# Attention with two exponential engines: own exponential buffers, more VectorE sets, and a sliding activity floor

## The chip, the cores and the metric

The kernel runs on one core of one Trainium2 chip. Its time is the device time of one execution in microseconds (us); the median of several executions is given. The profile is one execution taken by the hardware profiler. Its engines are TensorE (PE: matmuls, with weight loads shown apart as PEld), VectorE (DVE), ScalarE (ACT), GpSimd (POOL) and SyncE (SP). Each has its own instruction queue, and the instructions of a queue run in the order in which they were written. SBUF is the on-chip memory of 128 partitions, PSUM the memory into which TensorE writes, here eight banks of 512 float32 columns.

## The reference

For x of 2048 rows and 640 columns (bfloat16) the kernel computes a gated mix of an attention and a dense layer:

```python
g = sigmoid((x * gate_w).sum(-1, keepdims=True))
# A: 32 heads of 20 columns
q, k, v = split(x @ wqkv)
a = softmax(q @ k.T * 20 ** -0.5) @ v   # per head, 2048 x 2048 scores
a = concat(a) @ wo
# B: 640 -> 1536 -> 640
h = x @ w1 + b1
b = (h * tanh(softplus(h))) @ w2        # Mish
out = g * a + (1 - g) * b
```

The 32 heads have 2048 x 2048 scores each, 134 million exponentials in all, and they are the largest single piece of work.

## The kernel before

**Units, groups and sets.** A group G is a set of four heads (p, eight of these) with one chunk of 512 queries (qc, four of these), so there are 32 groups. In a group the keys come in 16 blocks of 128 (j). A unit is one head, one key block and 512 queries: a matmul of 32 rows (a head's 20 columns padded to 32, line 1051) writes the scores of 128 keys by 512 queries into one PSUM bank. Units are taken in order, alternately three and two at a time (`WIDTHS`), into two PSUM tiles S0 (three banks) and S1 (two banks). ScalarE then takes one exponential of the whole tile (`emit_exp`, line 1061) and writes it as bfloat16 into an SBUF tile E. The four units of one key block form a set: four matmuls of 21 columns (20 of V and one of ones, line 1107, `emit_set`) add into the single PSUM accumulator `acc`. After 16 sets a group is finished, and VectorE transposes the accumulator (line 1076), divides by the sums and transposes back.

The E tiles of both widths come from one pool `ep` with four buffers of 1536 columns. An exponential may write when the PV matmuls (line 1107) that read the tile four exponentials back are done.

**JV sets.** In the groups of `JV_GROUPS` (4 to 30 except multiples of 4, 20 groups) the last key block does not go to ScalarE. Its four score matmuls (line 682, `jv_chain`) write into ordinary PSUM banks, VectorE takes each over into `E_dve` (line 691), and seven VectorE operations on 2048 columns (lines 710 to 732, `jv_steps`) compute the exponential from its bits and a polynomial. The PV matmuls of this set (with `VB` as weights) are placed by `emit_jv` when the planner holds the result for ready. There is one `E_dve`, so a group's JV set has to be multiplied before the next group's is started.

**Other work.** The projections for Q, K and V, the dense layer with its Mish function, the output projection and a test of bounds are cut into chains: a list of matmul pieces, and an eviction by VectorE at the end. All share two PSUM banks (pool `pp`). The Mish of each of 48 tiles has an exponential on ScalarE (line 502) and a chain of VectorE operations.

**Order.** The order is written out by hand in the program itself, by a planner that runs while the kernel is built. It keeps an estimated time for each engine (`T`). For each exponential i it writes the scores of i + 1, the exponential i, the PV sets that are ready (`emit_pv`), VectorE steps that are due (`run_slow`) and then calls `pump`. That takes pieces of the chains in the order of their due times, hard ones 12 exponentials ahead of soft ones. [...]

**Filler matmuls.** `pump` also writes matmuls without use (`busy_matmul`, line 992), which multiply a constant tile `busy` (128 x 512 ones) by itself into a bank that is free. Their number is set by an account `owed`: each exponential adds 0.56 of 446 ns for each unit, less weights for its score and PV matmuls; every piece or filler takes its cost off. Above 110 ns something is written.

Of the kernel before, what the change touches and what calls it, by code (L numbers as in the profile page):

```python
# [9 lines left out]
P = 128  # L10
# [3 lines left out]
BF16 = mybir.dt.bfloat16  # L14
# [2 lines left out]

class Chain:  # L20

    def __init__(self, start, due, pieces, finish, ready=None, hard=True, bank=None):
        self.start, self.due, self.pieces, self.finish = start, due, deque(pieces), finish
        self.ready = ready or (lambda: True)
        self.hard = hard
        self.bank = bank
        self.fresh = True
        self.cost = sum(c for c, _ in pieces)  # L30

# [8 lines left out]
def attention_with_maximum(tc, A_wqkv, b_dram, out2d, xT, VA, wo_sb, g_t, ident, pool):  # L40
# [10 lines left out]
    with tc.For_i(0, H, 1, name="heads") as h:  # L51
# [20 lines left out]
        with tc.For_i(0, S, P, name="queries") as q0:  # L72
            q = pool["m"].tile([P, P], BF16, tag="e", name="q")
            nc.vector.tensor_copy(out=q[0:DH, :], in_=qT[0:DH, bass.ds(q0, P)])
            s0 = pool["s"].tile([P, 3 * QC], F32, tag="S0", name="s0")
            s1 = pool["s"].tile([P, QC], F32, tag="S1", name="s1")
            for c in range(S // QC):
                nc.tensor.matmul(
                    (s0[:, c * QC : (c + 1) * QC] if c < 3 else s1[:, :]),
                    lhsT=q[0:DH, :], rhs=kT[0:DH, c * QC : (c + 1) * QC], start=True, stop=True,  # L80
                )
            mx = pool["m"].tile([P, 4], F32, tag="r", name="mx")
            nc.vector.tensor_reduce(out=mx[:, 0:1], in_=s0, op=ALU.max, axis=X)
            nc.vector.tensor_reduce(out=mx[:, 1:2], in_=s1, op=ALU.max, axis=X)
            nc.vector.tensor_tensor(out=mx[:, 2:3], in0=mx[:, 0:1], in1=mx[:, 1:2], op=ALU.max)
            nc.vector.tensor_scalar(
                out=mx[:, 3:4], in0=mx[:, 2:3], scalar1=-scale, scalar2=None, op0=ALU.mult
            )
            e0 = pool["e"].tile([P, 3 * QC], BF16, tag="E", name="e0")
            e1 = pool["e"].tile([P, QC], BF16, tag="E", name="e1")  # L90
            for e, sc in ((e0, s0), (e1, s1)):
                nc.scalar.activation(e[:, :], sc[:, :], ACT.Exp, bias=mx[:, 3:4], scale=scale)
            eT = pool["stage"].tile([P, NS, P], BF16, tag="stage", name="eT")
            for b in range(0, NS, 8):
                ps = pool["pp"].tile([P, 8, P], BF16, tag="pp", name="ps")
                for j in range(8):
                    k = (b + j) * P
                    src = e0[:, k : k + P] if k < 3 * QC else e1[:, k - 3 * QC : k - 3 * QC + P]
                    nc.tensor.transpose(ps[:, j, :], src, ident)
                nc.vector.tensor_copy(out=eT[:, b : b + 8, :], in_=ps[:, :, :])  # L100
            o = pool["acc"].tile([P, DH + 1], F32, tag="acc", name="o")
            for j in range(NS):
                nc.tensor.matmul(
                    o[:, :], lhsT=eT[:, j, :], rhs=vh[:, j, :], start=(j == 0), stop=(j == NS - 1)
                )
            on = pool["m"].tile([P, DH], BF16, tag="h", name="on")
            rec = pool["t"].tile([P, 1], F32, tag="rec", name="rec")
            nc.vector.reciprocal(out=rec, in_=o[:, DH : DH + 1])
            nc.vector.tensor_scalar(
                out=on, in0=o[:, 0:DH], scalar1=rec, scalar2=None, op0=ALU.mult  # L110
            )
            nc.sync.dma_start(out=o_dram[bass.ds(q0, P), bass.ds(col, DH)], in_=on)

    with tc.For_i(0, NS, 1, name="rows") as s:
        op = pool["e"].tile([P, H, 32], BF16, tag="E", name="op")
        nc.vector.memset(op, 0.0)
        rows = bass.ds(s * P, P)
        nc.sync.dma_start(
# [5 lines left out]
        for p in range(NQ):  # L124
            nc.tensor.transpose(
                ps[:, p, :], op[:, 4 * p : 4 * p + 4, :].rearrange("p h d -> p (h d)"), ident
            )
        oT = pool["e"].tile([P, NQ, P], BF16, tag="E", name="oT")
        nc.vector.tensor_copy(out=oT[:, :, :], in_=ps[:, :, :])
        a = pool["s"].tile([P, 2, QC], F32, tag="S1", name="a")  # L130
        for half in range(2):
# [5 lines left out]
                )  # L137
        g = pool["t"].tile([P, 1], F32, tag="rec", name="g")
        nc.vector.tensor_copy(out=g, in_=g_t[:, bass.ds(s, 1)])
        ot = pool["e"].tile([P, 2, D // 2], BF16, tag="E", name="ot")  # L140
        nc.vector.scalar_tensor_tensor(
            out=ot[:, :, :], in0=a[:, :, 0 : D // 2], scalar=g,
            in1=bt.rearrange("p (a c) -> p a c", a=2), op0=ALU.mult, op1=ALU.add,
# [5 lines left out]
def kernel(  # L149
# [25 lines left out]
    LN2 = 0.6931471805599453  # L175
    Q_SCALE = 512.0 * float(DH) ** -0.5 / LN2
    WIDTHS = (3, 2)
    JV_GROUPS = [G for G in range(4, 31) if G % 4 != 0]
    JV_BIAS = 32
    N_CAP = 1.0e9  # L180
    NCELL = 48
    CELLS_KEPT = 2
# [12 lines left out]
    wsp = ctx.enter_context(tc.tile_pool(name="wsp", bufs=2))  # L195
    ktp = ctx.enter_context(tc.tile_pool(name="ktp", bufs=2))
    qtp = ctx.enter_context(tc.tile_pool(name="qtp", bufs=3))
    ep = ctx.enter_context(tc.tile_pool(name="ep", bufs=4))
    tp = ctx.enter_context(tc.tile_pool(name="tp", bufs=1))
    mp = ctx.enter_context(tc.tile_pool(name="mp", bufs=2))  # L200
    outp = ctx.enter_context(tc.tile_pool(name="outp", bufs=2))
# [12 lines left out]
    wkp = [consts.tile([P, KT, 4, 32], BF16, tag=f"wkp{i}", name=f"wkp{i}") for i in range(2)]  # L214
    T2 = [consts.tile([P, QC], BF16, tag=f"T2_{i}", name=f"T2_{i}") for i in range(2)]
    cells = [consts.tile([P, QC], BF16, tag=f"cell{i}", name=f"cell{i}") for i in range(NCELL)]
    busy = consts.tile([P, QC], BF16, tag="busy")
    xn = consts.tile([P, NQC], F32, tag="xn")
    wn = consts.tile([P, NQ, 2], F32, tag="wn")
    vn = consts.tile([P, 3], F32, tag="vn")  # L220
# [139 lines left out]
    def open_bank():  # L360
        T["pe"] = max(T["pe"], bank_free.popleft())
        bank_free.append(T["pe"])

    spare = [None]

# [310 lines left out]
    def jv_chain(G, p, t, start, due):  # L676
        box = {}
        bank = opener(box, QC)

        def piece():  # L680
            jv_free[0] = False
            nc.tensor.matmul(  # L682
                bank()[:, :],
                lhsT=kT[p][32 * t : 32 * t + 32, JV * P : (JV + 1) * P],
                rhs=qT[G][32 * t : 32 * t + 32, :],
                tile_position=(32 * t, 0),
            )

        def finish():
            evac(690)  # L690
            nc.vector.tensor_scalar(  # L691
                out=E_dve.bitcast(I16)[:, t, :], in0=box["ps"][:, :], scalar1=ROUND,
                scalar2=ROUND - 512.0 * JV_BIAS, op0=ALU.add, op1=ALU.subtract,
            )
            if t == 3:
                left = (it_at(G + 1) - now[0]) * 1115.0
                steps(T["dve"], jv_steps(G), T["act"] + left - 4000.0)

        def ready():
            return G in qT and (jv_free[0] if t == 0 else not jv_free[0])  # L700

        return Chain(start, due, [(215, piece)], finish, ready, bank=bank)

    def jv_steps(G):
        V = nc.vector
# [166 lines left out]
    for G, (p, qc) in enumerate(groups):  # L872
        if with_jv[G]:
            for t in range(4):
                x = it_at(G) + 3 + 3 * t
                chains.append(jv_chain(G, p, t, x, x + 3))

    def spread(a, b, n):
        return [(a + (b - a) * k / n, a + (b - a) * (k + 1) / n) for k in range(n)]
# [67 lines left out]
        ], x + 12, x + 24,  # L947
    ))
    chains.append(bound_chain(it_at(27), it_at(28)))
    chains.sort(key=lambda ch: (ch.due - (12 if ch.hard else 0), ch.start))  # L950
    shares = list(chains)

    current = [None]
    done = [0.0]
    BURST = 700.0
    UNIT = 446.0
    FLOOR = 0.56
    W_QK, W_PV = 0.5, 1.1
    AHEAD = 1500.0

    def run_piece():
        ch = current[0]
        cost, fn = ch.pieces.popleft()
        fn()
        T["pe"] += cost
        ch.fresh = False
        done[0] += cost
# [12 lines left out]
    def urgent(i):  # L980
        if current[0] is not None and current[0].hard and current[0].due <= i + 1:
            return True
        return any(ch.hard and ch.due <= i + 1 for ch in chains)

    def busy_matmul(ch):
        if ch is None:
            spare[0] = take_bank()
# [1 line left out]
        else:  # L989
            ps = ch.bank()  # L990
        n = ps.shape[1]
        nc.tensor.matmul(ps[:, 0:n], lhsT=busy[:, 0:P], rhs=busy[:, 0:n], start=True, stop=True)  # L992
        T["pe"] += n / 2.4
        return n / 2.4

    owed = [0.0]

    def pump(i, sets):
        want = sum(ch.share(i + 1) for ch in shares)
        if i >= 8:  # L1000
            owed[0] += FLOOR * UNIT * iters[i][1] - 215.0 * (W_QK + W_PV * sets)

        limit = T["act"] + NS_EXP[iters[min(i + 1, NI - 1)][1]] - NS_SCORES_SEEN - 60.0
        spent = 0.0
        while True:
# [2 lines left out]
            ch = current[0]  # L1008
            soon = ch is not None and urgent(i)
            must = soon or (ch is not None and done[0] < want and spent < BURST)  # L1010
            if not must and owed[0] < 110.0:
                break
            if not soon and (T["pe"] + 215.0 > limit or ((ch is None or ch.fresh) and not bank_ready())):
                break
# [4 lines left out]
            else:  # L1019
                break  # L1020
            spent += cost
            owed[0] = max(owed[0] - cost, -300.0)
        owed[0] = min(owed[0], 400.0)

    def run_later(i):
        go = sorted(x for x in later if x[0] <= i)
# [13 lines left out]
    def emit_qk(i):  # L1040
# [4 lines left out]
        S_of[i] = ps  # L1045
        T["pe"] = max(T["pe"], S_free.get(tag, 0.0))
        S_full[i] = T["pe"] + NS_SCORES_SEEN
        T["pe"] += NS_SCORES
        for k in range(n):
            G, p, qc, j, t = units[a + k]  # L1050
# [6 lines left out]

    def emit_exp(i):
        a, n = iters[i]
        E = ep.tile([P, max(WIDTHS) * QC], BF16, tag="E", name="E")  # L1060
        nc.scalar.activation(  # L1061
            E[:, 0 : n * QC], S_of.pop(i)[:, 0 : n * QC], ACT.Exp, scale=LN2 / 512.0
        )
# [39 lines left out]
    def emit_set(G, p, qc, j, moving, full, VB=None):  # L1103
        n = pv_sets[0]
        T["pe"] = max(T["pe"], full, T["acc"] if n == 0 else 0.0) + NS_SET
        for t in range(4):
            nc.tensor.matmul(  # L1107
                acc[32 * t : 32 * t + DH + 1, :],
# [54 lines left out]
    ]  # L1163
    def spin_up(n):
        for _ in range(n):
            nc.tensor.matmul(acc[:, :], lhsT=busy[:, 0:P], rhs=busy[:, :], start=True, stop=True)

    def first_proj(w, dst, ps, c0, n, eng):
        for kt in range(KT):
# [117 lines left out]
    with tc.If(ok == 0):  # L1287
        attention_with_maximum(
            tc, A_wqkv, b_dram, out2d, xT, VA, wo_sb[0], g_t, ident,
            dict(s=spool, acc=accpool, pp=pp, k=ktp, q=qtp, w=wsp, e=ep, stage=stage, t=tp, m=mp),  # L1290
        )
# [1 line left out]
_INS = ['A_x', 'A_wqkv', 'A_wo', 'B_x', 'B_w1', 'B_b1', 'B_w2', 'gate_w']  # L1293
# [26 lines left out]
```

## Time and profile before

| What | Value |
|---|---|
| median of three runs | 956.92 us (956.92, 956.92, 958.97) |
| profiled execution, its own time | 956.99 us |
| its span, first to last instruction | 955.1 us |
| mean granted TensorE clock | 0.991 |
| busy: ACT, PE, DVE | 925.8, 833.2, 637.9 us |
| exponentials of three and of two banks | 394 and 393 |
| filler matmuls recorded | 213 |
| JV sets | 20 of 512 sets |

A row of the groups of instructions reads: line, engine, operation, tile written <- tiles read, shapes, count, then busy time in us and the mean duration of one in ns, then the idle time of the engine just before these instructions and what ended most of it. In a row of the timeline the first two numbers are the start and the duration in us. Durations of instructions that follow each other closely on one engine overlap in the records, so busy time is less than their sum. A small part of the matmuls is missing from the record. The clock row gives the TensorE clock in tenths of full speed for each of 40 slices of the span.

### The profile page before, as it was taken

The numbers are of one execution on the slowest core, as the hardware profiler recorded it, in microseconds if no ns is written. First come the engines' busy times: TensorE is split into PE (matmuls) and PEld (weight loads), VectorE is DVE, ScalarE is ACT, GpSimd is POOL, SyncE is SP. The second block draws the span as 40 slices with busy tenths as digits, with TensorE's granted clock in tenths as the row PEclk, the third lists the DMA queues.
The fourth block names the chain that finished last, engine by engine and source line by source line (L and its number), as shares of the span: only waits on it lengthen the run. The fifth ranks groups of instructions, "written<-read, shape, count | busy, mean of one in ns | idle before, by whom it ended". The sixth has DMA issues, their size and how long they took to land.

```text
span 955.1 us, 14986 instructions
## 1 busy us (share of the span) xinstructions
PE 833.2 (87%) x5980; PEld 302.9 (32%) x6064; DVE 637.9 (67%) x1079; ACT 925.8 (97%) x841; POOL 22.0 (2%) x35
## 2 busy tenths in 40 slices
PE   8989888888888888888888888888899888899996
PEld 4433333222333233323332223322223233333332
DVE  4326576688747888678776787577784775755543
ACT  6999999999999999999999999999999999999995
POOL 5000010000000000000000000000000000000000
PEclk9999999999999999999999999999999999999998
DMA  9000100001000100001102001010000000000100
GB/s 285 11 1 1 30 1 22 22 1 30 2 1 21 30 1 22 1 2 49 30 9 48 1 1 30 14 37 14 8 1 21 1 2 15 35 15 15 39 25 29
DMA packets 25633, 21.97 MB, mean 23 GB/s; under 512 B 10088, under 2 KB 24312, under 8 KB 25560
## 3 DMA queue, kind: packets, MB, share of 16 engines
q1 hardware_dynamic: 22808, 14.28, 5.6%
q0 software_dynamic: 1520, 5.94, 1.9%
q8 instruction: 48, 0.79, 0.3%
q10 hardware_dynamic: 1232, 0.76, 0.3%
q14 instruction: 25, 0.20, 0.1%
HBM read 15.73 MB, written 5.24 MB: 22 GB/s over the span
## 4 chain that ended last, share of the span: by engine, by line
ACT 51%; issue 32%; PE 14%; DVE 1%; DMA 1%; POOL 1%; ACTq 0%; POOLq 0%
ACT E L1061 49%; PE Sp L1051 4%; PE acc L1107 3%; ACT e L502 2%; PE ps L592 2%; PE ps L637 2%; DMA wv<-in_A_wqkv_dram 1%; PE ps L561 1%; PE ps L444 1%; PE ps L682 0%; DVE ot L1270 0%; DVE T L1076 0%; POOL xs L266 0%; PE ps L778 0%; PE ps L992 0%
## 5 line engine op out<-in xcount | busy, mean ns | idle before, releaser
L1061 ACT ACTIVATE E<-Sp 128x1536 bf16<-128x1536 f32 (+1 forms) x787 | 904.4, 1265 | 10.9 <-PE acc L1107 6.1
L1051 PE MATMUL Sp<-qT,kT 32*128 32x512 bf16 x1968 | 310.8, 383 | 99.7 <-ACT E L1061 84.3
L1051 PEld LDWEIGHTS <-kT 32*128 32x128 bf16 x1968 | 113.1, 91 | 310.1 <-issue 284.9
L1107 PE MATMUL acc<-E,VA 128*21 128x512 bf16 x1968 | 195.8, 388 | 2.2 <-DVE T L1076 1.9
L1107 PEld LDWEIGHTS <-VA 128*21 128x21 bf16 x1968 | 48.4, 88 | 114.0 <-issue 113.7
L572 DVE TENSOR_SCALAR h<-ps,b1f 128x512 f32<-128x512 f32 x48 | 36.0, 751 | 65.9 <-PE ps L561 64.6
L592 PE MATMUL ps<-w_sb,cell 128*128 128x320 bf16 x384 | 76.3, 306 | 0.2 <-issue 0.2
L992 PE MATMUL ps<-busy 128*128 128x512 bf16 (+1 forms) x213 | 70.2, 386 | 1.1 <-issue 0.8
L561 PE MATMUL ps<-xT,w1t 128*128 128x512 bf16 x213 | 69.4, 385 | 1.7 <-issue 1.6
L691 DVE TENSOR_SCALAR E_dve<-ps 128x512 int16<-128x512 f32 x80 | 54.5, 684 | 12.8 <-PE ps L682 12.4
L444 PE MATMUL ps<-xT,wkp 128*128 128x512 bf16 x141 | 45.5, 384 | 2.8 <-issue 1.3
L637 PE MATMUL ps<-wo_sb,cell 128*128 128x320 bf16 x248 | 47.0, 302 | 0.0
L524 DVE RECIPROCAL r<-r 128x128 f32<-128x128 f32 x48 | 45.4, 947 | 0.8
L444 PE MATMUL ps<-xT,wqp 128*128 128x512 bf16 x136 | 43.4, 384 | 1.5 <-issue 1.3
L592 PEld LDWEIGHTS <-cell 128*128 128x128 bf16 x384 | 30.0, 98 | 35.5 <-issue 28.9
L455 DVE TENSOR_SCALAR qT<-ps 128x512 bf16<-128x512 f32 x31 | 21.4, 690 | 29.6 <-PE ps L444 28.4
L510 DVE SCALAR_TENSOR_TENSOR e<-e 128x512 f32<-128x512 f32 x48 | 32.7, 680 | 11.4 <-ACT e L502 11.2
L1076 DVE STREAM_TRANSPOSE T<-acc 128x512 f32<-128x512 f32 x32 | 22.9, 716 | 25.5 <-PE acc L1107 25.2
L604 DVE TENSOR_SCALAR Bt<-ps,g_t 128x320 bf16<-128x320 f32 x32 | 17.5, 548 | 31.9 <-PE ps L592 31.9
L459 DVE CAST kT<-ps 128x512 bf16<-128x512 f32 x31 | 21.3, 686 | 26.2 <-PE ps L444 25.2
L485 DVE CAST VA<-ps 128x80 bf16<-128x80 f32 (+2 forms) x48 | 16.4, 377 | 29.8 <-PE ps L472 29.6
L533 DVE TENSOR_TENSOR e<-e,r 128x512 f32<-128x512 f32 x48 | 33.2, 692 | 1.6
(107 smaller groups left out, 651.2 us busy)
## 6 DMA issues: line engine op xcount, KB each, us to landing
w1t<-in_B_w_dram SPq DMA_DIRECT2D x14, 480.0 KB, 3.8
b_dram<-Bt SPq DMA_DIRECT2D x4, 640.0 KB, 3.1
out_dram<-ot SPq DMA_DIRECT2D x14, 160.0 KB, 1.8
xs<-in_A_x_dram POOLq DMA_DIRECT2D x3, 640.0 KB, 7.5
w_sb<-in_B_w_dram POOLq DMA_DIRECT2D x1, 1920.0 KB, 12.4
ws<-in_A_wqkv_dram SPq DMA_DIRECT2D x13, 100.0 KB, 4.0
w1t<-in_B_w_dram POOLq DMA_DIRECT2D x2, 480.0 KB, 8.6
wo_sb<-in_A_wo_dram SPq DMA_DIRECT2D x4, 200.0 KB
```

Source lines behind the costliest of these rows:

```text
L444: nc.tensor.matmul(box["ps"][:, :], lhsT=wpad[:, kt, :, :].rearrange("p h d -> p (h d)"), rhs=xT[:, kt, chunk * QC : (chunk + 1) * QC], st ...
L524: V.reciprocal(out=r[:, Q], in_=r[:, Q])
L533: V.tensor_tensor(out=e.rearrange("p (a b) -> p a b", a=2), in0=e.rearrange("p (a b) -> p a b", a=2), in1=r[:, P : 3 * P].unsqueeze(1).to_ ...
L561: nc.tensor.matmul(box["ps"][:, :], lhsT=w1t[4 * c + ft // 3][:, kt, (ft % 3) * P : (ft % 3 + 1) * P], rhs=xT[:, kt, c * QC : (c + 1) * QC ...
L572: nc.vector.tensor_scalar(out=h, in0=box["ps"][:, :], scalar1=b1f[:, ft : ft + 1], scalar2=None, op0=ALU.add)
L592: nc.tensor.matmul(box["ps"][:, :], lhsT=act[(ft, c)][:, u * P : (u + 1) * P], rhs=w2_sb[:, ft, half * HALF : (half + 1) * HALF], start=(f ...
L637: nc.tensor.matmul(box["ps"][:, :], lhsT=OT[(p, c)][:, u * P : (u + 1) * P], rhs=wo_sb[0][:, p, cols], start=(k == 0), stop=(k == len(ps_l ...
L691: nc.vector.tensor_scalar(out=E_dve.bitcast(I16)[:, t, :], in0=box["ps"][:, :], scalar1=ROUND, scalar2=ROUND - 512.0 * JV_BIAS, op0=ALU.ad ...
L992: nc.tensor.matmul(ps[:, 0:n], lhsT=busy[:, 0:P], rhs=busy[:, 0:n], start=True, stop=True)
L1051: nc.tensor.matmul(ps[:, k * QC : (k + 1) * QC], lhsT=kT[p][32 * t : 32 * t + 32, j * P : (j + 1) * P], rhs=qT[G][32 * t : 32 * t + 32, :] ...
L1061: nc.scalar.activation(E[:, 0 : n * QC], S_of.pop(i)[:, 0 : n * QC], ACT.Exp, scale=LN2 / 512.0)
L1107: nc.tensor.matmul(acc[32 * t : 32 * t + DH + 1, :], lhsT=VA[:, j, 4 * p + t, :] if VB is None else VB[:, 4 * p + t, :], rhs=moving(t), st ...
```

## The change

1. The exponential tiles get two pools: `ep0` with three buffers of 1536 columns for S0 and `ep1` with two buffers of 1024 columns for S1, in place of four of 1536 (13,312 bytes of a partition in place of 12,288).
2. The tile `busy` shrinks to 128 x 128, and filler matmuls read one column of it 512 times (a broadcast with stride 0).
3. JV sets are made in all 27 groups from 4 to 30. Their chains are no longer hard, have a lead of 24 exponentials in the sorting, and are scheduled from one exponential after the group's start, two apart, in place of three and three.
4. `owed` gives way to `activity`: the planner notes the estimated start, the length and a weight of each matmul it writes (a group of scores 0.5, a PV set 1.1, every chain piece and filler 1.0), and sums them over the last 3413 ns. A filler or an early piece is written only while the sum is at or under 0.54.

The path with a row maximum, `attention_with_maximum`, takes the new pools; it is there for inputs outside the bounds and does not run here.

```diff
-    def __init__(self, start, due, pieces, finish, ready=None, hard=True, bank=None):
+    def __init__(self, start, due, pieces, finish, ready=None, hard=True, bank=None, lead=0):
...
+        self.lead = lead + (12 if hard else 0)
...
-    JV_GROUPS = [G for G in range(4, 31) if G % 4 != 0]
+    JV_GROUPS = list(range(4, 31))
     JV_BIAS = 32
+    LEAD_JV = 24
...
-    ep = ctx.enter_context(tc.tile_pool(name="ep", bufs=4))
+    ep = [
+        ctx.enter_context(tc.tile_pool(name="ep0", bufs=3)),
+        ctx.enter_context(tc.tile_pool(name="ep1", bufs=2)),
+    ]
...
-    busy = consts.tile([P, QC], BF16, tag="busy")
+    busy = consts.tile([P, P], BF16, tag="busy")
...
+    PERIOD = 3413.0
+    recent = deque()
+
+    def worked(start, ns, weight):
+        recent.append((start, ns, weight))
+        while recent[0][0] < start - 3 * PERIOD:
+            recent.popleft()
+
+    def activity(end):
+        return sum(
+            w * max(0.0, min(end, t + ns) - max(end - PERIOD, t)) for t, ns, w in recent
+        ) / PERIOD
...
-        return Chain(start, due, [(215, piece)], finish, ready, bank=bank)
+        return Chain(start, due, [(215, piece)], finish, ready, hard=False, bank=bank, lead=LEAD_JV)
...
-                x = it_at(G) + 3 + 3 * t
-                chains.append(jv_chain(G, p, t, x, x + 3))
+                x = it_at(G) + 1 + 2 * t
+                chains.append(jv_chain(G, p, t, x, x + 2))
...
-    chains.sort(key=lambda ch: (ch.due - (12 if ch.hard else 0), ch.start))
+    chains.sort(key=lambda ch: (ch.due - ch.lead, ch.start))
...
-    UNIT = 446.0
-    FLOOR = 0.56
-    W_QK, W_PV = 0.5, 1.1
+    FLOOR = 0.54
...
     def run_piece():
         ch = current[0]
         cost, fn = ch.pieces.popleft()
         fn()
+        worked(T["pe"], cost, 1.0)
         T["pe"] += cost
...
+    def busy_row(n):
+        return busy[:, 0:1].to_broadcast([P, n])
...
-        nc.tensor.matmul(ps[:, 0:n], lhsT=busy[:, 0:P], rhs=busy[:, 0:n], start=True, stop=True)
+        nc.tensor.matmul(ps[:, 0:n], lhsT=busy[:, :], rhs=busy_row(n), start=True, stop=True)
+        worked(T["pe"], n / 2.4, 1.0)
...
-        if i >= 8:
-            owed[0] += FLOOR * UNIT * iters[i][1] - 215.0 * (W_QK + W_PV * sets)
+        tag = f"S{i % len(WIDTHS)}"
...
-            if not must and owed[0] < 110.0:
+            if not must and (i < 8 or activity(max(T["pe"], S_free[tag])) > FLOOR):
                 break
...
-            owed[0] = max(owed[0] - cost, -300.0)
-        owed[0] = min(owed[0], 400.0)
...
+        worked(T["pe"], 215.0, 0.5)
         T["pe"] += NS_SCORES
...
-        E = ep.tile([P, max(WIDTHS) * QC], BF16, tag="E", name="E")
+        which = i % len(WIDTHS)
+        E = ep[which].tile([P, WIDTHS[which] * QC], BF16, tag=f"E{which}", name="E")
...
         T["pe"] = max(T["pe"], full, T["acc"] if n == 0 else 0.0) + NS_SET
+        worked(T["pe"] - NS_SET, 215.0, 1.1)
```

## The prediction

> **What bounds the kernel now.** I read the page's busy shares first, then the groups by shape, then the waits, and last narrow stretches around the places where ScalarE stood.
>
> ```profile
> span 955.1 us, 14986 instructions
> PE 833.2 (87%) x5980; PEld 302.9 (32%) x6064; DVE 637.9 (67%) x1079; ACT 925.8 (97%) x841; POOL 22.0 (2%) x35
> PEclk9999999999999999999999999999999999999998
> ```
>
> ScalarE carries the span. Its groups, with shapes kept apart, and its waits:
>
> ```profile
> L1061 ACT ACTIVATE E<-Sp 128x1536 bf16<-128x1536 f32 x394 | 581.3, 1475 | 9.2 <-PE acc L1107 6.1 <-PE Sp L1051 2.8 <-ACT E L1061 0.2
> L1061 ACT ACTIVATE E<-Sp 128x1024 bf16<-128x1024 f32 x393 | 414.7, 1055 | 1.8 <-PE Sp L1051 1.7
> L502 ACT ACTIVATE e<-h 128x512 f32<-128x512 f32 x48 | 31.6, 659 | 0.0
> ```
>
> The durations overlap by some 150 ns, so the price of an exponential is the distance from its start to the next start. I took it from the starts in the trace, as medians: 1330 ns for three banks, 904 for two, 519 for the Mish exponential. The sum is 394 x 1.330 + 393 x 0.904 + 48 x 0.5195 = 904.2 us. The exponentials run from 11.3 to 944.0 us, which is 932.7 us, so ScalarE stands for 28 us, though the idle column shows 11: a start that is late by less than the overlap is no idle time. Exponential by exponential (late by over 25 ns), 26.4 us are found, and by the last release before the start they divide so: three-bank exponentials behind PV matmuls (L1107) 17.8 us in 92 places, behind score matmuls 4.4; two-bank ones behind score matmuls 3.2 and behind PV 0.2; others 0.9. The commonest case is 125 to 136 ns, about every fourth pair. One of them, in the matmul rows of a stretch:
>
> ```profile
> 143.00 0.39 PE L1051 MATMUL Sp<-qT,kT 32*128 32x512 bf16 x3 [0.20 <-ACT E L1061]
> 143.32 0.40 PE L1107 MATMUL acc<-E,VA 128*21 128x512 bf16 x4
> ```
>
> The scores were there at 143.39, and the three-bank exponential started at 143.81, 83 ns after PV ended at 143.72. A PV set takes four units and reaches over exponentials, so the buffer of the one four back was read last by a set that also needs the one two back.
>
> The other loss is the TensorE clock, which falls to half for 3.41 us three times inside the run. Stretches of 3.41 us before and at each fall (columns: busy time of PE, PEld, DVE, ACT and POOL, clock):
>
> ```profile
> 204.86:208.28 3.42, 2.30 (x20) 0.74 (x17) 2.91 (x5) 3.42 (x5) 0.00 (x0) 1.00 0.00 0
> 208.28:211.69 3.41, 3.41 (x15) 0.64 (x13) 3.20 (x7) 2.67 (x3) 0.00 (x0) 0.50 0.00 0
> ...
> 491.58:495.00 3.42, 2.44 (x26) 1.22 (x26) 2.63 (x6) 3.42 (x5) 0.00 (x0) 1.00 0.00 0
> 495.00:498.41 3.41, 3.41 (x21) 0.95 (x21) 2.84 (x6) 2.72 (x3) 0.00 (x0) 0.50 0.00 0
> 689.55:692.97 3.42, 2.47 (x18) 0.71 (x17) 2.98 (x6) 3.42 (x4) 0.00 (x0) 1.00 0.00 0
> 692.97:696.38 3.41, 3.41 (x18) 0.84 (x18) 3.24 (x7) 2.49 (x3) 0.00 (x0) 0.50 0.00 0
> ```
>
> In each slow stretch one exponential comes late, by 0.92, 1.08 and 1.07 us. The sum below is made against this execution's span, 955.1 us; its own time was 956.99, 1.9 more, and the median of the three runs is 956.92.
>
> **Fewer exponentials.** Seven more groups (4, 8 ... 28) give four units each to VectorE: 1968 units become 1940, 394 and 393 exponentials become 388 and 388. That takes off 6 x 1.330 + 5 x 0.904 = 12.5 us. By the page's busy time per unit, 904.4 / 1968 = 0.46, it would be 28 x 0.46 = 12.9. I take 12.5.
>
> **Own buffers.** The three-bank exponential then waits for the sets of the one six back; the two-bank one still for four back, and that wait cost 0.2 us. Of the 17.8 us, 2.0 lie in two of the clock falls, and 2.5 lie between 846 and 932 us, where PE is busy 72.9 of 75 us and score matmuls stand right behind (35 to 116 ns late in their own places). So 17.8 - 2.0 - 2.5 = 13.3 us go. Bounds: 9, if the cases above 300 ns (a PV set late behind the transpose of the accumulator) stay, and 17.8. What is late next is the score matmul.
>
> **VectorE's work.** 28 more evictions at 684 ns are 19.2 us, and seven chains of 689 + 686 + 1216 + 692 + 693 + 1222 + 1222 = 6.42 us are 45.0, together 64 us. With row durations laid on the written order, groups 4 to 30 hold 642 us of VectorE work (578 before) for 746 us of ScalarE pitch, 86%; the fullest is group 17 with 26.2 of 26.5. The free seventh hides it. In the written order (of the built programs) the last JV step still stands 1 to 3 exponentials before its PV set, and the set mostly 2 to 8 exponentials farther from the group's end than before. Price 0; bounds 0 and +4 (twice the two late groups before, 0.83 and 1.28 us at 541.96 and 658.63). JV score matmuls, 28 more, 384 ns each, lie in PE's gaps of 99.7 us before scores; each takes one of the two banks for its 684 ns eviction, and no PE row waits for a bank now.
>
> **The constant row.** In the written order there are 246 filler matmuls instead of 237, nine at about 0.22 us, in the same gaps. The trace has no matmul that reads one element 512 times. By the filler's row (388 ns each) the price is 0; a full array that took double would add 246 x 0.216 = 53 us on PE, against 99.7 us of waiting gaps. I take 0, since rows with the same size differ by at most a few ns in the trace whatever tensors they read. SP's loads, POOL's copies: the same number; some w1 loads stand two or three places apart from before, each landing in 3.8 us with a tile of lead.
>
> **The activity floor.** What makes the clock fall? I weighted every matmul's streaming time (512 columns are 216 ns from one full matmul to the next): full ones 1, a 32-row score matmul 1/6, a 21-column PV matmul 0.275, and summed over a grid of 3.413 us, on which all three falls lie (84 and 58 steps apart). Of 273 stretches the three before a fall have the lowest sums: 0.30, 0.32 and 0.35. If a JV score matmul counted 1, as the new planner counts it, two of them would have 0.40 and 0.43, with 10 and 21 stretches at full clock below them. So the true floor is near 0.35, and JV matmuls hardly help. In the written order of the changed kernel they stand closer: in group 4, three of four come within two exponentials with no full matmul between, and no filler is put there because the planner sees activity. Laying both orders along the exponentials' pitch, a grid of any phase finds on average 2.0 stretches below 0.35 before (three were) and 10.5 after; in 14 places the sum goes under 0.30, down to 0.17. So I expect some 7.5 more falls. One costs between 0.4 us (scores alone are late: at 208.28 they would have allowed 0.37) and 1.1; with a third buffer I take 0.8, so +6.0.
>
> [...]
>
> **Sum.** 955.1 - 12.5 - 13.3 + 0 + 6.0 = 935.3 us of span; with 1.9 around it, 937.
>
> **Rivals.**
> (A) As summed, 0.50: 937, its own range 931 to 946.
> (B) The floor over a sliding period does its work after all, no fall is added and the old three go, 0.22: 955.1 - 12.5 - 13.3 - 3.1 (0.92, 1.08, 1.07) + 1.9 = 928. For it: the mean sum rises from 0.525 to 0.535, and fillers come where the last 3.4 us were thin. Against it: JV matmuls' full weight.
> (C) VectorE becomes the bound in some groups, 0.12: if VectorE runs late and PE waits for it in half of 27 groups, at 1.05 us (the mean of 0.83 and 1.28), +14: 951. For it: 26.2 of 26.5 us in group 17, 26.8 of 27.8 in group 4. Against: VectorE's own waits are nearly all for PE, and no PV set waited for a JV result.
> (D) Slower: the gate does not count matmuls that read a row of stride 0, 0.08. With fillers at weight 0, 45 stretches fall below 0.35, 42 more than three, at 0.9 us: 955.1 - 12.5 - 13.3 + 38 + 1.9 = 969. It decides from about 30 added falls. For it: nothing shows how the gate counts; against: the filler of before, constant ones too, must have counted, since without it 38 stretches would lie below 0.35.
> (E) Own buffers do nothing, the wait moves whole to scores, 0.08: 955.1 - 12.5 + 6.0 + 1.9 = 950.5. Against: scores were ready 0.4 us earlier at 143.39.
>
> **How the numbers follow.** The time is A's, 937. From B (928) to C and E (951) the range leaves out D and A's far ends: 927 to 951. No change within 0.3%, about what a measurement of this kernel can tell, means 954.0 to 959.8. A, B, E and most of C lie below: 0.88. Same 0.04, slower 0.08.
>
> **What would show it.** After: 388 and 388 exponentials at 1330 and 904 ns; the three-bank group's idle time behind PV near zero (was 6.1 us); VectorE near 702 us; between 8 and 14 stretches at half clock, most just after JV score matmuls, the surest in group 4, some 120 us in; filler matmuls at 388 ns. Wrong if the clock falls over 30 times, if PV sets wait for JV results, or if three-bank exponentials wait for scores where they had waited for PV.

## The result

The changed kernel takes 948.25 us in the median of six executions (940.37 to 954.20); the kernel before takes 957.94 (954.15 to 961.41). The ratio is 0.9874 with a 95% interval of 0.9826 to 0.9922, so it is faster by about 10 us. The forecast was 937, with a range of 927 to 951. Executions more than 1.5% above the fastest of the same kernel are not counted, here or below, which leaves out one, 964.19 us of the version with common buffers.

The profiled execution is the slowest of the six, 954.20 us with a span of 952.3. First the page:

```profile
span 952.3 us, 14757 instructions
PE 863.2 (91%) x6073; PEld 298.8 (31%) x6073; DVE 694.3 (73%) x1156; ACT 912.2 (96%) x830; POOL 21.7 (2%) x35
PEclk9999997979999999979999999999999989999998
```

VectorE has 56 us more work, ScalarE's busy time is 14 us less, and the clock row has dents that the row of before had not. The groups by shape, and ScalarE's first wait:

```profile
L1081 ACT ACTIVATE E<-Sp 128x1536 bf16<-128x1536 f32 x388 | 607.8, 1567 | 6.4 <-PE Sp L1070 5.8
L1081 ACT ACTIVATE E<-Sp 128x1024 bf16<-128x1024 f32 x388 | 440.6, 1136 | 15.5 <-PE Sp L1070 15.0
L1014 PE MATMUL ps<-busy 128*128 128x512 bf16 x246 | 75.5, 389 | 0.0
```

The waits behind PV are gone from the three-bank row (they were 6.1 us of its idle time), the distances from start to start are still 1331 and 904 ns at the median, and what ScalarE waits for now is scores. Done again exponential by exponential, the lateness is 35.7 us, where before had 26.4: none of it behind PV, 32.6 behind scores (two-bank ones 21.8, three-bank ones 10.8) and the rest unassigned. Of the 35.7 us, 23.9 fall in or just behind stretches of half clock, 11.8 elsewhere.

The clock falls nine times inside the run, to exactly half, but the slow time is 64.9 us, that is 19 stretches of 3.413 us and not nine: the first fall lasts five of them. Stretches around it (busy time of PE, PEld, DVE, ACT and POOL with the number of instructions, then the clock, the busy share of the DMA engines and the GB/s that they moved):

```profile
135.09:138.50 3.41, 2.58 (x23) 0.83 (x20) 3.41 (x8) 3.41 (x5) 0.00 (x0) 1.00 0.54 134
138.50:141.91 3.41, 2.40 (x11) 0.64 (x10) 3.21 (x7) 3.22 (x3) 0.00 (x0) 0.50 0.36 70
141.91:145.33 3.42, 3.42 (x19) 0.62 (x17) 1.70 (x3) 2.17 (x2) 0.00 (x0) 0.50 0.00 0
145.33:148.74 3.41, 3.41 (x17) 0.66 (x13) 2.27 (x4) 2.67 (x3) 0.00 (x0) 0.50 0.01 2
...
152.15:155.57 3.42, 3.42 (x18) 0.94 (x15) 2.25 (x3) 2.42 (x2) 0.00 (x0) 0.50 0.01 2
155.57:158.98 3.41, 3.41 (x26) 1.03 (x25) 2.57 (x3) 3.23 (x5) 0.00 (x0) 1.00 0.00 0
```

And what PE did in the stretch before the fall:

```profile
L1070 PE MATMUL Sp<-qT,kT 32*128 32x512 bf16 x7 | 1.4, 377 | 0.5 <-ACT E L1081 0.5
L1128 PE MATMUL acc<-E,VA 128*21 128x512 bf16 x12 | 1.2, 386 | 0.0
L702 PE MATMUL ps<-qT,kT 32*128 32x512 bf16 x3 | 0.9, 380 | 0.0
L581 PE MATMUL ps<-xT,w1t 128*128 128x512 bf16 x1 | 0.4, 390 | 0.0
```

Three of the four JV score matmuls of group 4 stand there, one full matmul, and no filler. The other eight falls are alike: in the stretch before each, two or three JV score matmuls start and no filler.

The six executions differ by 14 us, three at 940 to 943 and three at 954, so none lies near the median. Their mean clock goes with them: 0.984 in the fastest (span 938.5), 0.962 in the slowest. With every fall to half, as in the profile, slow time is 2 x (1 - clock) x span, an estimate of 30 against 72 us, which is 12.4 stretches for 13.8 us: 1.1 us each. In the profiled one 23.9 us of lateness over 19 stretches are 1.26 each.

### The profile page after: what moved, and what is told of

It reads as the page before. It is cut to its first block, busy times and chain, and to the rows that moved or that the text cites. A ratio compares the mean times of both kernels' runs of the same rounds, so it can differ in the third digit from the quotient of the medians.

```text
span 952.3 us, 14757 instructions
## 1 busy us (share of the span) xinstructions
PE 863.2 (91%) x6073; PEld 298.8 (31%) x6073; DVE 694.3 (73%) x1156; ACT 912.2 (96%) x830; POOL 21.7 (2%) x35
## 4 chain that ended last, share of the span: by engine, by line
ACT 61%; issue 18%; PE 18%; DVE 1%; DMA 1%; POOL 1%; ACTq 0%; POOLq 0%
ACT E L1081 58%; PE Sp L1070 5%; PE acc L1128 3%; ACT e L522 3%; PE ps L657 2%; PE ps L612 2%; PE ps L581 2%; PE ps L464 2%; DMA wv<-in_A_wqkv_dram 1%; PE ps L702 1%; PE ps L1014 0%; PE ps L492 0%; DVE ot L1291 0%; DVE h L592 0%; POOL xs L272 0%
## 5 line engine op out<-in xcount | busy, mean ns | idle before, releaser
L1081 ACT ACTIVATE E<-Sp 128x1536 bf16<-128x1536 f32 (+1 forms) x776 | 894.5, 1351 | 21.9 <-PE Sp L1070 20.8
L1070 PEld LDWEIGHTS <-kT 32*128 32x128 bf16 x1940 | 104.0, 91 | 306.4 <-issue 287.9
L711 DVE TENSOR_SCALAR E_dve<-ps 128x512 int16<-128x512 f32 x108 | 71.8, 678 | 12.7 <-PE ps L702 12.3
L581 PE MATMUL ps<-xT,w1t 128*128 128x512 bf16 x240 | 80.3, 406 | 0.0
L1014 PE MATMUL ps<-busy 128*128 128x512 bf16 x246 | 75.5, 389 | 0.0
L464 PE MATMUL ps<-xT,wkp 128*128 128x512 bf16 x155 | 49.1, 405 | 1.7 <-DVE xT L430 0.8
L464 PE MATMUL ps<-xT,wqp 128*128 128x512 bf16 x155 | 48.4, 392 | 0.0
L702 PE MATMUL ps<-qT,kT 32*128 32x512 bf16 x108 | 38.3, 387 | 0.0
L522 ACT ACTIVATE e<-h 128x512 f32<-128x512 f32 x48 | 35.5, 739 | 0.7 <-DVE h L592 0.7
(107 smaller groups left out, 694.3 us busy)
```

The lines of the kernel that those rows point to most:

```text
L464: nc.tensor.matmul(box["ps"][:, :], lhsT=wpad[:, kt, :, :].rearrange("p h d -> p (h d)"), rhs=xT[:, kt, chunk * QC : (chunk + 1) * QC], st ...
L522: nc.scalar.activation(e[:, :], h[:, :], ACT.Exp)
L581: nc.tensor.matmul(box["ps"][:, :], lhsT=w1t[4 * c + ft // 3][:, kt, (ft % 3) * P : (ft % 3 + 1) * P], rhs=xT[:, kt, c * QC : (c + 1) * QC ...
L702: nc.tensor.matmul(bank()[:, :], lhsT=kT[p][32 * t : 32 * t + 32, JV * P : (JV + 1) * P], rhs=qT[G][32 * t : 32 * t + 32, :], tile_positio ...
L711: nc.vector.tensor_scalar(out=E_dve.bitcast(I16)[:, t, :], in0=box["ps"][:, :], scalar1=ROUND, scalar2=ROUND - 512.0 * JV_BIAS, op0=ALU.ad ...
L1014: nc.tensor.matmul(ps[:, 0:n], lhsT=busy[:, :], rhs=busy_row(n), start=True, stop=True)
```

## The experiments

The theory after the result: own buffers and fewer exponentials give what was forecast, and the thin order around JV matmuls lets the clock fall, for more stretches at a time than forecast. Rivals: the row of stride 0 does not count as activity; VectorE's added work makes the scores late; the own buffers gave nothing.

**A filler ahead of each JV matmul.** A full matmul goes into the JV matmul's own bank just before it, so no bank is waited for.

```diff
         def piece():
             jv_free[0] = False
+            nc.tensor.matmul(bank()[:, :], lhsT=busy[:, :], rhs=busy_row(QC), start=True, stop=True)
             nc.tensor.matmul(
...
-        return Chain(start, due, [(215, piece)], finish, ready, hard=False, bank=bank, lead=LEAD_JV)
+        return Chain(start, due, [(430, piece)], finish, ready, hard=False, bank=bank, lead=LEAD_JV, weight=0.58)
...
-        worked(T["pe"], cost, 1.0)
+        worked(T["pe"], cost, ch.weight)
```

> The changed kernel, with one filler matmul written into a JV matmul's own bank just before it (108 more fillers in all), counted by the planner as 430 ns at weight 0.58. Theory (thin JV stretches let the clock fall): the written order has on average 0.3 stretches of 3.41 us under 0.35 where the changed kernel has 10.5; 0 to 2 falls, lateness of exponentials from 35.7 us to about 12 to 14 us, time 926 to 933 in every execution, and the executions lie within 3 us of each other. Rival (VectorE's added work makes scores late): falls may go, but the late scores stay and 108 fillers add to PE: 945 to 955. Rival (a row of stride 0 does not count as activity): added fillers do nothing, 945 to 955 with 8 or more falls.

934.65 us (934.14 to 936.62), ratio to before 0.9739 (0.9695 to 0.9784). The profiled execution has one fall of one stretch, and the other five have a mean clock of 0.997, which leaves room for little more than the slow end that every profile here has. The lateness in slow stretches goes from 23.9 to 1.3 us, so the falls are what the changed kernel lost, and this version beats both kernels. Its clock row has lost the dents:

```profile
PEclk9999999999999999999999999999999999999998
```

The time is 2 us above the theory's 926 to 933: at full clock 17.3 us of lateness are left, not 12 to 14. In nine groups two pairs of filler and JV matmul stand in a row ahead of the scores, and a two-bank exponential is 422 to 510 ns late for it; here PE's rows of the timeline:

```profile
476.98 0.39 PE L703 MATMUL ps<-busy 128*128 128x512 bf16 x1
477.30 0.39 PE L704 MATMUL ps<-qT,kT 32*128 32x512 bf16 x1
477.62 0.39 PE L703 MATMUL ps<-busy 128*128 128x512 bf16 x1
477.94 0.38 PE L704 MATMUL ps<-qT,kT 32*128 32x512 bf16 x1
477.95 1.04 PE L1072 MATMUL Sp<-qT,kT 32*128 32x512 bf16 x5
```

The two-bank exponential at 478.64 is 429 ns late.

**The JV matmul's weight in the planner.**

```diff
-        return Chain(start, due, [(215, piece)], finish, ready, hard=False, bank=bank, lead=LEAD_JV)
+        return Chain(start, due, [(215, piece)], finish, ready, hard=False, bank=bank, lead=LEAD_JV, weight=1 / 6)
...
-        worked(T["pe"], cost, 1.0)
+        worked(T["pe"], cost, ch.weight)
```

> The changed kernel with a JV matmul noted by the planner at weight 1/6 in place of 1, nothing else. Theory (the planner's wrong weight keeps fillers away): the order has 288 fillers for 246 and 6.3 stretches under 0.35 for 10.5, since the JV matmuls stay bunched and hold the banks; 4 to 7 falls, 8 to 14 slow stretches, 938 to 944. Rival (the weight is right and the falls have another cause): no change within the scatter, 940 to 954. Rival (stride 0 does not count): no change.

938.98 us (937.47 to 940.44), ratio 0.9783 (0.9737 to 0.9828). Three falls and seven slow stretches, one fewer of each than the theory had, with 9.0 us of lateness in them. By the medians the wrong weight is about nine of the 13.6 us between 948.25 and 934.65. Before each of the three falls left, two JV matmuls and no filler stand in the stretch; the theory puts that down to bunched JV matmuls that hold the banks, which no run tests by itself.

**Fillers that read different data.**

```diff
-        nc.tensor.matmul(ps[:, 0:n], lhsT=busy[:, :], rhs=busy_row(n), start=True, stop=True)
+        nc.tensor.matmul(ps[:, 0:n], lhsT=busy[:, :], rhs=xT[:, 0, 0:n], start=True, stop=True)
```

> The changed kernel with the filler matmuls reading 512 different columns of x (stride 1, real data) in place of one column of ones 512 times; the instructions stand in the same order. Theory (falls come from the order, the row is without effect): 7 to 11 falls, time 940 to 954 like the changed kernel, filler matmuls at 385 to 390 ns. Rival (a row of stride 0 does not count as activity, or only in part): falls back to 3 or fewer, 926 to 935.

947.25 us (944.48 to 953.75), six falls and 16 slow stretches: one fall fewer than the theory's 7 to 11, and far from the rival's 926 to 935. The fillers' mean is 397 ns, since 14 of 246 run at half clock (6 in the changed kernel); at full clock it is 383 ns in both. So in this kernel the row of stride 0 shows no cost (383 ns a filler in both, 947.25 against 948.25 us), and with real data in its place the falls do not go to three or fewer: nothing here tells the two apart as activity.

**The common exponential buffers again**, four of 1536 columns, in the changed kernel.

> The changed kernel with the four common exponential buffers of before, everything else as changed. Theory (own buffers took away 17.8 us of waits behind PV): three-bank exponentials wait for PV matmuls again, 12 to 18 us in some 90 places; at full clock that is added in whole, in slow stretches part of it hides behind late scores: 952 to 968. Rival (own buffers do nothing, the wait only changes its name): the time of the changed kernel, 940 to 954.

952.16 us (948.34 to 958.42), ratio to before 0.9932 (0.9891 to 0.9973). This lies in both ranges and does not decide between them; the profile does. The wait is back: three-bank exponentials are late behind PV by 17.3 us in 105 places, 15.3 of it at full clock. The median rises by only 4 us over the changed kernel's 948.25, but the changed kernel's executions had more slow time: three of its six had a mean clock of 0.962, and here none was under 0.967. At a mean clock of 0.980 the changed kernel took 941.56 us and this version 949.32; at 0.979 and 0.978 they took 942.92 and some 952: 8 to 9 us more. In the profile's waits of ScalarE (time in us, number, longest):

```profile
ACT E L1078 <- PE Sp L1067: 8.9, 17, 1.0
ACT E L1078 <- PE acc L1125: 5.5, 17, 1.2
```

**Own buffers in the kernel before**, alone (with the row of stride 0, which makes room for them).

> The kernel before with only the two pools of exponential buffers (3 and 2) and the row of stride 0 that makes room for them; 20 JV groups and the old account of fillers, so every instruction stands in the order of before. Theory (own buffers take the wait behind PV away and hardly anything takes its place at full clock): lateness of three-bank exponentials behind PV from 17.8 to under 2 us, behind scores up from 7.6 to 9 to 12 us, 2 to 5 falls of the clock, 12 to 16 us faster than before, 942 to 947. Rival (the wait moves to the scores): 954 to 959.

947.07 us (946.40 to 949.06), ratio 0.9851 (0.9809 to 0.9893), 11.8 us less, just short of the theory's 12 to 16 and far from the rival. Some of it is not the buffers: the executions of the kernel before that were taken along had a mean clock of 0.976 to 0.993, these 0.991 to 0.994. Where before had 0.992 and 0.993 it took 954.15 to 956.82, this version 947.47 and 947.61: 7 to 9 us. Behind PV 0.03 us are left, and behind scores 13.6 came where 7.6 had been, with one fall of two stretches among them. ScalarE's row:

```profile
L1065 ACT ACTIVATE E<-Sp 128x1536 bf16<-128x1536 f32 x394 | 651.1, 1653 | 3.4 <-PE Sp L1054 3.2
```

This one part of the change, with 20 JV groups, is as fast as the whole change.

**JV sets in 27 groups in the kernel before**, alone.

```diff
-    JV_GROUPS = [G for G in range(4, 31) if G % 4 != 0]
+    JV_GROUPS = list(range(4, 31))
```

> The kernel before with JV sets in all 27 groups and nothing else: four common buffers, old schedule of the JV chains, old account of fillers. Theory (JV matmuls are thin, and the planners count them full, the old one too): 12.5 us less of exponentials; 7.5 stretches under 0.35 in the order where before has 2.0, so 5 to 9 falls, 8 to 16 slow stretches at 1.0 to 1.3 us each against 3: 948 to 956. Rival (the new floor makes the falls, not the JV sets): 2 to 4 falls, 944 to 947.

995.02 us (991.77 to 999.59), 3.4% slower than before: both expectations were far off. There are nine falls and 30 slow stretches, but beside them four exponentials come 4.5, 5.4, 7.5 and 8.2 us late behind PV matmuls. Eight times PE waits for the accumulator's transpose, for 23.1 us in all:

```profile
PE acc L1107 <- DVE T L1076: 23.1, 8, 5.7
PE acc L1107 <- DVE E_dve L732: 2.8, 2, 1.8
```

The largest case, in VectorE's rows of the timeline, from the last step of the JV set to the transpose:

```profile
536.00 1.23 DVE L732 TENSOR_TENSOR E_dve<-E_dve,w_dve 128x2048 int16<-128x2048 int16 x1
537.14 0.68 DVE L510 SCALAR_TENSOR_TENSOR e<-e 128x512 f32<-128x512 f32 x1
537.86 0.43 DVE L511 TENSOR_SCALAR r<-e 128x512 f32<-128x512 f32 x1
...
541.28 0.69 DVE L533 TENSOR_TENSOR e<-e,r 128x512 f32<-128x512 f32 x1
542.01 0.69 DVE L542 TENSOR_TENSOR cell<-h,e 128x512 bf16<-128x512 f32 x1
542.62 0.71 DVE L1076 STREAM_TRANSPOSE T<-acc 128x512 f32<-128x512 f32 x1
```

Its PV set runs at 537.28, the group's last; the transpose that frees the accumulator stands behind a whole Mish chain of nine operations (the first begun before the set), and the next exponential starts 8.2 us late, at 544.08. The code says why. A JV set that is not ready when its group ends is forced in by `emit_pv` with `run_slow(float("inf"))`, and that writes out every VectorE step that waits, Mish steps too, ahead of the transpose. In the trace of this version groups 4, 7, 11 and 16 have five to eight VectorE operations between the start of the last PV set and the transpose, which begins 3.0 to 5.0 us after that set; in the changed kernel it begins 0.35 us after it at the most. In each of the four places the clock falls too.

**The old JV schedule in the changed kernel** (hard, no lead, three exponentials apart, from the third).

```diff
-        return Chain(start, due, [(215, piece)], finish, ready, hard=False, bank=bank, lead=LEAD_JV)
+        return Chain(start, due, [(215, piece)], finish, ready, bank=bank)
...
-                x = it_at(G) + 1 + 2 * t
-                chains.append(jv_chain(G, p, t, x, x + 2))
+                x = it_at(G) + 3 + 3 * t
+                chains.append(jv_chain(G, p, t, x, x + 3))
```

> The changed kernel with the old schedule of the JV chains (hard, no lead of 24, from three exponentials after the group's start, three apart), all else as changed. Theory (with 27 groups VectorE has no room, and a JV set that is not ready is forced in as its group's last set, for which the planner writes out every waiting VectorE step ahead of the accumulator's transpose): the order has 7 or 8 VectorE operations between JV result and transpose in groups 10, 16, 17 and 22; there PE waits for the transpose 5 to 6 us and ScalarE stands 6 to 8 us; 2.8 stretches under 0.35, but each such stand lets the clock fall too: 960 to 985. Rival (the early schedule only bunches the JV matmuls and costs more than it gives): fewer falls than the changed kernel and no long stand, 934 to 942.

975.02 us (971.71 to 976.89), ratio 1.0154 (1.0096 to 1.0212), as the theory had it: ScalarE stands for 6.2, 10.9, 6.3 and 6.3 us, at the ends of four groups. The 10.9 us hold two waits of PE, 5.05 for the JV set's own result and 5.49 for the transpose. PE's waits:

```profile
PE acc L1128 <- DVE T L1096: 25.2, 8, 5.7
PE acc L1128 <- DVE E_dve L752: 7.8, 5, 5.1
```

So VectorE holds the kernel up at group ends as soon as the JV sets come late, and the early schedule is worth some 27 us here. By the written orders (10.5 thin stretches against 2.8 with the old schedule) it is also what bunches the JV matmuls.

**No fillers.** The floor is 0.

> The changed kernel with the floor at 0, so no filler matmul at all. Theory (the clock falls after a stretch of 3.41 us with a weighted sum under about 0.33 and comes back only after one over about 0.69): the order has 34 stretches under 0.35, and without fillers slow stretches seldom reach 0.69: 20 to 30 falls, 60 to 120 slow stretches of some 275, at 1.26 us each 1000 to 1080. Rival (only an idle stretch of 3.41 us lets the clock fall): PE is never idle that long, no more falls than now, 925 to 955.

1001.97 and 1013.37 us. Sixteen falls, fewer than the theory's 20 to 30, with 80 slow stretches and 73.7 us of lateness in them, 0.92 each. Its clock row:

```profile
PEclk9999955885599988999977986765899978999997
```

PE's longest gap here is 1.47 us, and it is busy for 1.65 to 2.61 us of the 3.41 before each fall, so the rival (only an idle stretch lets the clock fall) is out.

**The old account of fillers in the changed kernel.**

> The changed kernel with the old account of fillers (0.56 of 446 ns per unit, less the weights) in place of the sliding sum. Theory (the sliding sum is better than the account, the JV matmuls spoil both): 151 fillers for 246, 16.0 stretches under 0.35 for 10.5; 12 to 16 falls, 22 to 34 slow stretches at 1.26 us: 952 to 968. Rival (the sliding sum is what makes the falls): 3 falls or fewer, 932 to 938.

970.32 us (964.39 to 977.67), 2 us above the theory's range, ratio 1.0115 (1.0043 to 1.0187). Twelve falls and 34 slow stretches, 37.8 us of lateness in them. The sliding sum is worth 22 us against the account, though it counts JV matmuls wrongly.

**The filler and the JV matmul as two pieces, three exponentials apart.**

```diff
-        return Chain(start, due, [(430, piece)], finish, ready, hard=False, bank=bank, lead=LEAD_JV, weight=0.58)
+        return Chain(start, due, [(215, fill), (215, piece)], finish, ready, hard=False, bank=bank, lead=LEAD_JV, weight=0.58)
...
-                x = it_at(G) + 1 + 2 * t
+                x = it_at(G) + 1 + 3 * t
```

> The kernel with a filler ahead of each JV matmul, with the pair cut into two pieces of 215 ns (the planner tests whether a piece still fits before the next scores; the pair was tested with 215 and took 430), and the JV chains three exponentials apart in place of two. Theory (the 440 ns lateness once in most groups comes from two pairs in a row ahead of the scores, 1.28 us of PE): 0.2 stretches under 0.35, 0 to 1 falls, lateness from 17.3 to 10 to 14 us, 928 to 932. Rival (scores are late because VectorE's evictions hold the banks): 933 to 936.

957.36 us (951.59 to 963.36): both expectations were wrong, by 20 us and more. Two exponentials stand for 7.0 and 6.0 us, at 510.30 and 665.02 us, at the ends of groups 16 and 21, where the order has eight VectorE operations ahead of the transpose: the spacing of three makes the JV sets late. The clock falls during each, the first time for nine stretches.

**The same two pieces, two exponentials apart.**

> The kernel with a filler ahead of each JV matmul, in two pieces, at the changed kernel's own spacing of two exponentials. Theory (the loss of the version with spacing three came from JV sets forced in last in groups 16 and 21): no group has more than four VectorE operations between JV result and transpose, no stand above 1.5 us; late scores a little under the 17.3 us of the unsplit version; 0 to 1 falls, 930 to 934. Rival (splitting in itself holds a bank longer and makes scores late): 936 to 955.

938.46 us (935.43 to 944.33). No long stand, which settles what was wrong with the spacing of three. The time lies in the rival's range. But it is 4 us slower than the unsplit version and its clock goes from 0.983 to 0.997: some executions have falls again. In the one without any, the lateness is 18.2 us, hardly more than the 17.3 of the unsplit version, so there late scores, the rival's reason, cost little. Splitting gains nothing; why its falls vary from execution to execution was not looked into.

## Why the prediction was right, and what in it was wrong

The time lies in the range and on the forecast side, 11 us above the point. Term by term, for the profiled execution:

- **Fewer exponentials, -12.5.** Right: 388 and 388, at the same distances. Own buffers with 20 groups (947.07) and the 27-group version almost without falls (934.65) are 12.4 us apart, a loose check, since their falls and fillers differ too.
- **Own buffers, -13.3.** Right in mechanism, some 4 us too large. The 16.0 us behind PV at full clock went to zero, and other lateness at full clock rose from 7.4 to 11.8: -11.6 for the whole change. For the buffers alone, count all time at full clock by which exponentials start later than the distances 1330, 904 and 519.5 ns allow, also below the 25 ns of the other counts: 25.2 us before and 16.0 with own buffers added; 23.2 with common buffers in the changed kernel and 14.0 without. That is 9.2 us in both pairs, close to the lower bound of 9, and it agrees with the 7 to 9 us at like clock above. The prediction took 13.3 of the wait off and put nothing for scores that come late in its place. What is late next is the score matmul, as said; rival E is out.
- **VectorE, 0.** Right in size for this order (PE's waits for VectorE's transposes are 0.8 us), with 694.3 us busy for some 702. But its reason, that VectorE's free seventh hides the work, is not enough: with the old schedule the same work is there, and PE waits 25.2 us for transposes. The cover is the early schedule, whose effect the prediction saw in the written order without saying that the price rests on it. Rival C had the mechanism in part (PE waits for VectorE in some groups) and a price of 1.05 us; with the old schedule ScalarE stood 6 to 11 us each time, in four groups, since a whole Mish chain is written ahead of the transpose.
- **The constant row, 0.** Right: 389 ns, and reading other data changes nothing that can be told from the scatter (947.25 against 948.25 us). Rival D is out.
- **More falls, +6.0.** The step that was most mis-sized. The number of falls was near (9 against 10.5 expected), and so was the place: all come just after JV score matmuls, the first in group 4, at 138.5 us and not "some 120 us in". But the stretches at half clock were 19 in the profiled execution, not 8 to 14. The price was wrong: 0.8 us a fall, taken from falls of before that lasted one stretch each. These lasted 2.1 stretches on average at 1.26 us, 2.66 a fall, and the lateness in slow stretches rose from 3.1 to 23.9 us: +20.8 in place of +6.0.

With the measured terms 955.1 - 12.5 - 16.0 + 4.4 + 20.8 = 951.8, against a span of 952.3. By their mean clock the faster executions of the changed kernel had fewer slow stretches, about 6 in the fastest (an estimate: slow time as above, less the 8.3 us at the end of the run), and the median lies between. Rival B (no added falls), at 928, is near what the order would give without them: an estimate of 952.3 - 23.9 + 1.9 = 930. A filler per JV matmul, which stops the falls, reached 934.65.

One thing the prediction could not see in three executions of the kernel before: its falls vary as well. In the 17 taken along with own buffers alone it took 954.15 to 966.93 us at a mean clock of 0.993 to 0.976. By the slow time 955.15 and 966.93 us lie some 9.7 stretches apart, an estimate of 1.2 us each, the price found after the change and not 0.8. That the time came within the range owes something to luck: three of the six executions, at 954 us, lie outside it.

## What to carry to other kernels

Where an engine's exponentials alternate in width, give each width its own output buffers, and read lateness from start to start: the idle column showed 6.1 us of a wait that came to 17.8. And before pricing its removal look at what comes next: own buffers won 9 us here. A planner's weights decide where fillers go, so measure them against the clock in the trace; here a matmul of 32 rows counted as a full one, and none of the nine stretches before a fall had a filler. And when one engine is at 86% of another's time, look at what a late item pulls ahead of it in a queue: one forced flush cost 4 to 11 us each time.

## What the hardware showed that was not expected

In these profiles the clock fell after thin stretches and came back after ones with about twice the sum. For the twelve kernels here whose profile has a fall inside the run I summed the weighted streaming time (weights as in the prediction, time at the clock of the moment) over every stretch of the 3.413 us grid inside the run. The sums are estimates: the planner's 0.5 for a group of scores and 1.1 for a PV set give the weights, for three score and four PV matmuls, and no run measured them by themselves. The counts:

```
stretch at full clock, sum    stays at full    falls to half
under 0.32                          0               55
0.32 to 0.36                       36               18
over 0.36                         all                0

stretch at half clock, sum    returns to full  stays at half
under 0.64                          0               74
0.64 to 0.72                       16               76
over 0.72                          55                2
```

The counts near the borders move by a few with where in its record a matmul is placed, the borders themselves hardly. In the profiles of before and after alone, the twelve falls come after sums of 0.24 to 0.35, and the lowest sum without a fall is 0.33; ten stretches at half clock with 0.57 to 0.71 stay there, twelve with 0.67 to 0.81 return. In the changed kernel's profile full matmuls in a row start 398 to 427 ns apart at half clock, 215 at the least at full clock, so the same order has about twice the sum (an estimate from these two), and an order whose sum is near 0.33 at full clock comes to some 0.66, in the row where 76 of 92 stretches stayed slow. Of the five slow stretches in a row from 138.5 us four have sums of 0.59 to 0.70, and the last, 0.73, ends them. Before, each fall was followed by a dense stretch (0.67 to 0.69) and lasted one.

In the same two profiles every fall inside the run is to 0.50 and lasts one to five times 3.413 us. PE was not idle ahead of it: it was busy 2.58 of 3.41 us before the fall at 138.5, and in the version without fillers, with sixteen falls, its longest gap was 1.47 us.

A smaller thing: the recorded duration of an exponential is no price. With the waits behind PV gone the three-bank mean rose from 1475 to 1653 ns in the version with own buffers alone, while the median distance from start to start went from 1330 to 1337.
